# A fused attention, expert layer and convolution layer on one core: the first v split on GpSimd, DMA issues in another order, idle products in the routing, and a first copy in halves

## The chip, the cores and the metric

The kernel runs on one core of one Trainium2 chip. The metric is the device time of one execution in microseconds (us), the median of several runs. Five instruction streams run beside each other: TensorE (PE; its weight loads are shown apart as PEld), VectorE (DVE), ScalarE (ACT), GpSimd (POOL) and SyncE (SP), which here only issues DMA transfers. An instruction starts when those ahead of it in its own stream have been issued and the semaphores that it waits for have come. ACT and POOL issue DMAs too, each on its own queue (ACTq, POOLq; SP's is SPq).

## The reference, cut to what matters

Three layers follow each other. The attention has 4 batches of 8 heads, 576 positions and 64 columns, with a decay bias:

```python
scores = scale * np.matmul(q, k.transpose(0, 1, 3, 2))
cum = np.cumsum(np.maximum(s, 0.0), axis=-1)
bias = -(cum[:, :, :, None] - cum[:, :, None, :])
scores = np.where(causal, -1000000000.0, scores + np.minimum(bias, 0.0))
attn = exp(scores - max(scores));  attn = attn / (sum(attn) + 1e-09)
x = attn @ v                                   # heads joined: 4 x 576 x 512
logits, gate = x @ w_gate, sigmoid(x @ w_local)
e = argmax(logits[b, s]) if s == 0 or gate[b, s] < 0.5 else prev_e
y[b, s] = softmax(logits[b, s])[e] * (relu(x[b, s] @ w1[e]) @ w2[e])   # 8 experts, 512 -> 1024 -> 512
h = relu(y @ w_in);  out = (h * sigmoid(conv3(h))) @ w_out             # conv along s, 3 taps
```

Everything is float32. The kernel holds most operands as two float16 parts, a high one and the remainder.

## The kernel before

The attention goes through 8 units of 4 heads (`u` 0 to 7; two units are one batch). For each unit k and q come in by SP (`load`, tiles `st`), are split in high and low parts (`split_hi` on ACT, `split_lo` on GpSimd or DVE, tile `h` or in place in `st`), are transposed by two DMAs of SP (`turn`, written `k<-h` or `k<-st` in the trace) and copied into the second operand tile by DVE (`copy`, L290). `extra` lays the decay rows into the operand tile by two DMAs (`k<-ex`). There are three such operand tiles, `K1[0]` to `K1[2]`, and `constants` fills their constant rows by three memsets; `K1[2]` (named `k_143` in the order) first serves unit 2.

A unit needs a first pass, **stage a** (`za`, L391, reduced by DVE at L394 and L423), which finds each row's maximum. `max_turn` turns the maxima on PE (`mt`, L460), `max_out` copies them on ACT (`mr`, L465) and `max_row` writes them by DMA into a row of the operand tiles: two DMAs `k<-mr` (L472) for the heads' full blocks, one `t<-mr` (L475) for the last 64 positions, the tail. All went by SP, except the tail row of unit 0, which ACT issued. Only behind these can `scores` (`z`, L494 and L522) be taken; then come exp on ACT, the low part `plo` on DVE (L550) and the products with v (`o`, L566). Stage a of unit u+1 runs in pieces among the scores of unit u.

v comes in once for a batch by `loadv`: for batch 0 the first half (heads of unit 0) by GpSimd's queue, the second half (unit 1) by SP, 8 DMAs `nv` and 4 `nvt`. `split_v` (L337 on) scales v and takes the two parts `vv` and `vvt`, and a float32 copy `v0` of one block. For unit 0 ACT made the high parts (L351), DVE the low ones (L355) and GpSimd `v0`; for the later units GpSimd makes all, seven operations.

The order is written out by hand: every task gets a time in steps in `PAR` (`start` for the opening; `at` for the splits, transposes and extra rows of a unit, counted back from the unit's first step), and tasks are emitted sorted by it. On each engine the order of emission is the order of execution. `busy` puts out products that nobody reads, two ahead of each of the first eight scores.

Behind the attention `Routing.finish` picks an expert for each position: the last turned tile (`xT`, `xTt`), `logits` (L966, L971), the recurrence over positions (`nrp`, `rfp` on PE, a scan `er` on DVE, `ep` back on PE), ranks in each expert (`rk`), and index sums (`ix`, L1084) from which `rows` makes `idx`, the list of rows to gather. `warm` puts out products between (L1094, `w1` = 6 and `w2` = 8 of them). The expert layer works in blocks of 128 rows: `gather` (GpSimd, indirect, tile `xg`), `turn` (8 transposing products `xp` at L1258, one ACT copy `xt` at L1259), `mm1` (`hp`, L1228), `mm2`. ACT and DVE meanwhile split the experts' weights (tile `r`, L1159 and L1170). The last layer, `moe2`, follows.

Of the kernel before, what the change touches and what calls it, by code (L numbers as in the profile page):

```python
# [21 lines left out]
NB = 27  # L22
# [19 lines left out]
def bc(ap, shape):  # L42
    return ap.to_broadcast(shape)


class Keep:
# [7 lines left out]
 'u2': {'at': (-22.5, -21.5, -19, -18.9, -18), 'cp': (-14, -13), 'lv': -11, 'sv': -2, 'pa': -12, 'pn': 7, 'mx': -6},  # L54
 'u3': {'load': -35, 'loadq': 0, 'at': (-33, -30, -28, -27, -26.9), 'cp': (-22, -21), 'sv': -1, 'pa': -20, 'pn': 14, 'mx': -6},
# [52 lines left out]
           'ctq': 3.3,  # L108
           'c2': 3.5,
           'pt': 4.8,  # L110
           'mtt': 5.8,
           'sv0': 5.85,
           'mot': 5.9,
           'mrt': 5.95,
           'z': 6.0,
           'lv1': 7.5},
 'r': {'cut': 12, 'w1': 6, 'w2': 8, 'w3': 6},
# [7 lines left out]
def attention(tc, ctx, q, k, v, s, xd, rt, hook):  # L125
# [212 lines left out]
    def split_v(u):  # L338
        b, o = u // 2, u % 2 * NH
        a, t = U[b, "v"][:, o:o + NH], U[b, "vt"][:, o // 2:o // 2 + 2]  # L340
        w = U[u, "vv"] = vp.tile([128, NH, 4, 2, 65], F16, name="vv")
        wt = U[u, "vvt"] = vp.tile([128, NH // 2, 2, 65], F16, name="vvt")
        v0 = U[u, "v0"] = vp.tile([128, NH, 65], F32, name="v0")
        for x in (w, wt):
            i = (slice(None),) * (len(x.shape) - 2)
            G.memset(x[i + (0, slice(64, 65))], 1.0)
            G.memset(x[i + (1, slice(64, 65))], 0.0)
        G.memset(v0[:, :, 64:65], 1.0)
        for x, dh, dl in ((a, w[:, :, :, 0, 0:64], w[:, :, :, 1, 0:64]), (t, wt[:, :, 0, 0:64], wt[:, :, 1, 0:64])):
            if u == 0 or not PAR["h"]["vg"]:  # L350
                A.activation(dh, x, AF.Copy, scale=VS)  # L351
            else:
                G.tensor_scalar(dh, x, VS, 0.0, op0=ALU.mult, op1=ALU.add)
            if u == 0:
                V.scalar_tensor_tensor(dl, in0=x, scalar=VS, in1=dh, op0=ALU.mult, op1=ALU.subtract)  # L355
            else:
                G.tensor_scalar(x, x, VS, 0.0, op0=ALU.mult, op1=ALU.add)
                G.tensor_tensor(dl, x, dh, op=ALU.subtract)
        G.tensor_scalar(v0[:, :, 0:64], a[:, :, 0], VS if u == 0 else 1.0, 0.0, op0=ALU.mult, op1=ALU.add)
# [15 lines left out]
    def busy(z, n):  # L375
        for _ in range(n):
            PE.matmul(z.rearrange("p (x c) -> p x c", c=128), lhsT=id16, rhs=bc(id16[:, None], [128, 4, 128]), start=True, stop=True, skip_group_check=True)
# [89 lines left out]
    def max_row(u, hs=slice(0, 4), tails=True):  # L467
        n, Q = 0, nc.sync if u or hs else nc.scalar
# [15 lines left out]
    def scores(x):  # L484
# [4 lines left out]
        if 1 <= steps.index(x) <= 8:  # L489
            busy(z, 2)  # L490
# [194 lines left out]
    def second_a(r):  # L685
# [4 lines left out]
        lv0=lambda: loadv(0, 0, G), c2=lambda: (constants(G, K1[2]), tctx.close()),  # L690
# [101 lines left out]
class Routing:  # L792
# [210 lines left out]
    def finish(self, ctx, busy, between, behind):  # L1003
# [9 lines left out]
        z = T("z", [128, 512], pool=ps)  # L1013
        self.logits(NU - 1, z)
        self.collect(NU - 1)
        nrp, rfp = T("nrp", [128, 1024], pool=ps), T("rfp", [128, 1024], pool=ps)
# [4 lines left out]

        nrs, er = T("nrs", [128, S]), T("er", [128, S], F16)
# [22 lines left out]
        rk = T("rk", [128, 2, 8, 20], pool=ps)  # L1045
        PE.matmul(rk[:, 1], lhsT=self.ones, rhs=of, start=True, stop=True, skip_group_check=True)
        PE.matmul(rk[:, 0], lhsT=self.later, rhs=of, start=False, stop=True, skip_group_check=True)
        V.tensor_tensor(ex, ex, o, op=ALU.mult)
# [31 lines left out]
        ix, ixs = T("ix", [128, 5, NB], pool=ps), T("ixs", [128, 2, NB])  # L1080
# [153 lines left out]
def moe(tc, xd, yd, m, w_in, w_out, keep, splits, room, weights, xgp, xtp, unit):  # L1234
# [3 lines left out]
    with ExitStack() as ctx:  # L1238
# [14 lines left out]
        def turn(b):  # L1253
# [5 lines left out]
            A.activation(t, z, AF.Copy)  # L1259
# [409 lines left out]
```

## Time and profile before

| | |
|---|---|
| median of 3 runs | 684.68 us (684.28 to 685.42) |
| the profiled execution | 686.55 us, its span 684.3 us |
| PE busy | 623.9 us, 91% of the span |
| DVE busy | 451.0 us, 66% |
| ACT busy | 393.2 us, 57% |
| POOL busy | 255.4 us, 37% |
| attention, to the last turned tile | about 0 to 225 us |
| routing, to the first expert product | about 225 to 248 us |
| expert layer | about 248 to 508 us |
| last layer | about 508 to 684 us |

The span runs from the first to the last instruction on the core; 2.25 us of the profiled time lie around it. A busy share is an average over stages with different limits. In rows of the timeline "[2.98 <-DMA t<-mr]" says that the engine stood idle for 2.98 us ahead of this instruction, and what ended the wait. PEclk is TensorE's granted clock as a share of full speed; it has two levels, 1.2 GHz (0.50) and 2.4 GHz (1.00), so a mean between them is a stretch with both.

### The profile page before, as it was taken

To read this page: it belongs to the slowest core of one execution; us is meant where nothing else is said; L and a number is where in the kernel's file an instruction comes from. 1 tells how busy PE (TensorE), PEld (TensorE's weight loads), DVE (VectorE), ACT (ScalarE), POOL (GpSimd) and SP (SyncE) were. 2 spreads that over 40 slices of the span, in tenths; PEclk is the share of its full clock that TensorE was granted. 3 is DMA by queue.
4 is the path that set the end of the run, shared out by engine and by line. 5 is a ranking of instruction groups with operands and counts; after the bars stand their busy time and mean duration, and the time that the engine had idled before them with its cause. 6 is when DMAs were issued, how large, how long until landed. Compare 5 with 4: busy or idle time off the path is not lost. (4 is left out here: it accounts for less than half of the span.)

```text
span 684.3 us, 15451 instructions
## 1 busy us (share of the span) xinstructions
PE 623.9 (91%) x5177; PEld 390.1 (57%) x5177; DVE 451.0 (66%) x861; ACT 393.2 (57%) x661; POOL 255.4 (37%) x369
## 2 busy tenths in 40 slices
PE   6758899899999389899999989999899999999997
PEld 3437688778888244344444434444477766565443
DVE  7788888898765798475858486753059993645000
ACT  5656588687797837465637363632069975554111
POOL 8988966572350089612543434333000000000000
PEclk9989999999999689999999999999999999999999
DMA  7877866956655258999999999962471300000111
GB/s 173 169 163 132 151 141 129 156 101 137 219 146 214 60 185 234 249 364 235 263 353 192 335 175 238 202 152 67 104 128 29 71 16 32 16 31 32 47 61 48
DMA packets 168921, 101.80 MB, mean 149 GB/s; under 512 B 119808, under 2 KB 147112, under 8 KB 168828
## 3 DMA queue, kind: packets, MB, share of 16 engines
q1 hardware_dynamic: 164712, 88.65, 54.8%
q0 software_dynamic: 4112, 12.00, 5.8%
q8 instruction: 47, 0.77, 0.5%
q14 instruction: 46, 0.38, 0.2%
q10 hardware_dynamic: 4, 0.00, 0.0%
HBM read 62.18 MB, written 15.31 MB: 113 GB/s over the span
## 5 line engine op out<-in xcount | busy, mean ns | idle before, releaser
L1228 PE MATMUL hp<-r,xt 128*128 x504 | 113.9, 383 | 9.9 <-ACT xt L1259 8.1
L1228 PE MATMUL yp<-r,ht 128*128 x504 | 112.2, 379 | 1.6 <-PEq L1342 1.6
L1503 PE MATMUL o<-wo,g 128*128 128x512 f16 x432 | 94.5, 379 | 0.0
L1228 PEld LDWEIGHTS <-xt 128*128 128x128 f16 x504 | 49.6, 99 | 70.6 <-ACT xt L1259 11.3
L1455 PEld LDWEIGHTS <-wi 128*128 128x128 f16 x768 | 75.1, 98 | 21.9 <-issue 1.7
L1228 PEld LDWEIGHTS <-ht 128*128 128x128 f16 x504 | 48.6, 98 | 57.3 <-issue 2.6
L1170 DVE SCALAR_TENSOR_TENSOR r<-st,r 128x512 f32 (+3 forms) x80 | 71.0, 949 | 9.6 <-ACT r L1159 8.3
L1455 PE MATMUL hp<-yt,wi 128*128 128x288 f16 x576 | 71.9, 286 | 0.0
L1291 POOL DMA_INDIRECT yd<-ys,idx x21 | 21.9, 1044 | 132.0 <-DVEq L1212 77.1
L1159 ACT ACTIVATE r<-st 128x512 f32 (+3 forms) x84 | 57.4, 761 | 23.8 <-SPq L1221 16.0
L1503 PEld LDWEIGHTS <-g 128*128 128x128 f16 x432 | 42.3, 98 | 49.5
L538 ACT ACTIVATE phi<-z,lnes 128x512 f16<-128x512 f32 (+1 forms) x80 | 50.7, 634 | 34.1 <-PE z L497 33.7
L394 DVE TENSOR_REDUCE mx<-za 128x1 f32<-128x384 f32 (+4 forms) x93 | 54.5, 601 | 15.2 <-PE za L391 14.6
L550 DVE TENSOR_TENSOR plo<-z,phi 128x512 f16<-128x512 f32 (+1 forms) x80 | 48.1, 602 | 9.6 <-ACT z L539 8.1
L494 PE MATMUL z<-k 128*128 128x128 f16 (+2 forms) x320 | 48.6, 275 | 5.7 <-DVE plo L550 2.5
L539 ACT ACTIVATE z<-z,lnes 128x512 f32<-128x512 f32 (+1 forms) x80 | 48.7, 608 | 0.0
L1472 DVE SCALAR_TENSOR_TENSOR c<-hb,cw,c 128x576 f32<-128x576 f32 x32 | 26.1, 816 | 33.2 <-ACT c L1466 33.2
L1506 ACT ACTIVATE s<-o 128x512 f32<-128x512 f32 x18 | 10.7, 596 | 61.4 <-PE o L1503 61.4
L566 PE MATMUL o<-v,p 128*128 128x65 f32 x256 | 44.0, 283 | 0.0
L1289 ACT ACTIVATE ys<-yp,pp 128x512 f16<-128x512 f32 x21 | 14.4, 684 | 49.3 <-PE yp L1228 29.9
L1306 DVE TENSOR_SCALAR f<-s 128x256 int32<-128x256 int32 x32 | 11.6, 361 | 45.0 <-POOL wo L1315 16.1
L566 PE MATMUL o<-vv,phi 128*128 128x65 f16 (+1 forms) x512 | 41.1, 200 | 0.0
(299 smaller groups left out, 1236.5 us busy)
## 6 DMA issues: line engine op xcount, KB each, us to landing
st<-in_moe_w_dram SPq DMA_DIRECT2D x8, 2048.0 KB
st<-in_moe_w_dram SPq DMA_DIRECT2D x24, 512.0 KB
out_dram<-s SPq DMA_DIRECT2D x18, 256.0 KB
st<-in_k_dram SPq DMA_DIRECT2D x16, 256.0 KB
st<-in_q_dram SPq DMA_DIRECT2D x16, 256.0 KB
xd<-xh SPq DMA_DIRECT2D x16, 256.0 KB
k<-in_moe_w_dram SPq DMA_DIRECT2D x8, 512.0 KB
s<-in_moe_w_in_dram SPq DMA_DIRECT2D x16, 256.0 KB
```

The costliest lines, as they stand in the source:

```text
L394: return lambda: V.tensor_reduce(out, z.rearrange("p (e c) -> p e c", e=m), axis=AX.X, op=ALU.max)
L494: PE.matmul(out, lhsT=ks[i], rhs=qs[i], start=first and not i, stop=False, skip_group_check=True)
L538: A.activation(hi[:, 0:n], z[:, 0:n], AF.Exp, bias=lnes, scale=1.0 / SC)
L539: A.activation(p[:, 0:n], z[:, 0:n], AF.Exp, bias=lnes, scale=1.0 / SC)
L550: (V if md == "a" else G).tensor_tensor(lo[:, 0:n], p[:, 0:n], hi[:, 0:n], op=ALU.subtract)
L566: PE.matmul(out, lhsT=w, rhs=x, start=first, stop=last, skip_group_check=True)
L1159: i = self.nc.scalar.activation(hi, src, AF.Copy, scale=self.scale[w])
L1170: i = nc.vector.scalar_tensor_tensor(lo, in0=src, scalar=sc, in1=hi, op0=ALU.mult, op1=ALU.subtract)
L1228: i = self.nc.tensor.matmul(out, lhsT=lhsT, rhs=self.rings[w][:, c, k, bass.ds(s, 1), f], **kw)
L1455: PE.matmul(st[x][:, n, 0:HN], lhsT=wi[:, c, k, m], rhs=t[:, n, a + k], start=k + a + c == 0, stop=k == 3 and a == 4)
L1472: V.scalar_tensor_tensor(c, in0=h[:, 1:S + 1], scalar=cw[:, m, 1:2], in1=c, op0=ALU.mult, op1=ALU.add)
L1503: PE.matmul(o, lhsT=g[:, a, k, 128 * i:128 * i + 128], rhs=wo[:, c, k], start=j == 0, stop=j == 23)
```

## The change

Four things change.

- **The first v.** `split_v` puts all seven operations on GpSimd for unit 0 too; its task moves from 5.85 to 3.4. The memsets of `K1[2]` move behind the splits of unit 2 (`c3` at 6.6).
- **Issues in another order.** The tail row of unit 0 goes by SP. The second half of v is loaded at 5.98 instead of 7.5, the dump of zeros into `xd` at 8.0 instead of 6.0. Unit 2's extra rows go behind unit 1's maximum rows, unit 3's split of k behind the second v split.
- **Idle products.** `finish` puts out 3, 4, 5, 2 and 12 products into a tile `W` of its own, a whole PSUM bank that later holds `ix`; `w2` falls from 8 to 2. The eighth begin step has 5 `busy` products instead of 2.
- **The first copy.** `xt` of block 0 is copied in two halves.

```diff
- 'u2': {'at': (-22.5, -21.5, -19, -18.9, -18), 'cp': (-14, -13), ...
- 'u3': {'load': -35, 'loadq': 0, 'at': (-33, -30, -28, -27, -26.9), ...
+ 'u2': {'at': (-22.5, -21.5, -19, -18.9, -15.8), 'cp': (-14, -13), ...
+ 'u3': {'load': -35, 'loadq': 0, 'at': (-30.9, -30, -28, -27, -26.9), ...
...
+           'sv0': 3.4,
            'c2': 3.5,
+           'c3': 6.6,
...
-           'sv0': 5.85,
...
-           'z': 6.0,
-           'lv1': 7.5},
- 'r': {'cut': 12, 'w1': 6, 'w2': 8, 'w3': 6},
+           'lv1': 5.98,
+           'z': 8.0},
+ 'r': {'cut': 12, 'w1': 6, 'w2': 2, 'w3': 6},
...
-            if u == 0 or not PAR["h"]["vg"]:
-                A.activation(dh, x, AF.Copy, scale=VS)
-            else:
-                G.tensor_scalar(dh, x, VS, 0.0, op0=ALU.mult, op1=ALU.add)
-            if u == 0:
-                V.scalar_tensor_tensor(dl, in0=x, scalar=VS, in1=dh, op0=ALU.mult, op1=ALU.subtract)
-            else:
-                G.tensor_scalar(x, x, VS, 0.0, op0=ALU.mult, op1=ALU.add)
-                G.tensor_tensor(dl, x, dh, op=ALU.subtract)
+            G.tensor_scalar(dh, x, VS, 0.0, op0=ALU.mult, op1=ALU.add)
+            G.tensor_scalar(x, x, VS, 0.0, op0=ALU.mult, op1=ALU.add)
+            G.tensor_tensor(dl, x, dh, op=ALU.subtract)
...
-        n, Q = 0, nc.sync if u or hs else nc.scalar
+        n, Q = 0, nc.sync
...
-            busy(z, 2)
+            busy(z, 5 if steps.index(x) == 8 else 2)
...
+        W = T("ix", [128, 512], pool=ps)
+
+        def idle(n):
+            for _ in range(n):
+                PE.matmul(W.rearrange("p (x c) -> p x c", c=128), lhsT=self.id16, rhs=bc(self.id16[:, None], [128, 4, 128]), start=True, stop=True, skip_group_check=True)
+
+        idle(3)
         self.logits(NU - 1, z)
         self.collect(NU - 1)
+        idle(4)
...
+        idle(5)
...
+        idle(2)
         PE.matmul(rk[:, 1], lhsT=self.ones, rhs=of, start=True, stop=True, skip_group_check=True)
         PE.matmul(rk[:, 0], lhsT=self.later, rhs=of, start=False, stop=True, skip_group_check=True)
+        idle(12)
...
-        ix, ixs = T("ix", [128, 5, NB], pool=ps), T("ixs", [128, 2, NB])
+        ix, ixs = W[:, 0:5 * NB].rearrange("p (i n) -> p i n", n=NB), T("ixs", [128, 2, NB])
...
-            A.activation(t, z, AF.Copy)
+            for r in (slice(0, 4), slice(4, 8)) if b == 0 else (slice(0, 8),):
+                A.activation(t[:, r], z[:, r], AF.Copy)
```

On **SP**, between the transposes of unit 1 and those of unit 2 (tile `h` to `k`), the issues stood like this before. `k_142` is unit 1's operand tile, `k_143` unit 2's, `t_144` the tail's; `st` are the loads of k, q and k of units 2 and 3.

```order
L286 DMA k_142<-ex 3x2x1024 x2
L702 DMA xd<-zero 512x1x256
L170 DMA st_112<-in_k_dram 128x4x128 x2
L170 DMA st_112<-in_q_dram 128x4x128 x2
L170 DMA st_111<-in_k_dram 128x4x128 x2
L180 DMA nv<-in_v_dram 64x4x64 x8
L184 DMA nvt<-in_v_dram 32x2x64 x4
L282 DMA_TRANSPOSE k_717<-h 128x32x64 x2
L286 DMA k_143<-ex 3x2x1024 x2
L472 DMA k_142<-mr 1x8x128 x2
L475 DMA t_144<-mr 1x2x128
```

After, they stand like this.

```order
L287 DMA k_142<-ex 3x2x1024 x2
L470 DMA t_144<-mr 1x2x128
L181 DMA nv<-in_v_dram 64x4x64 x8
L185 DMA nvt<-in_v_dram 32x2x64 x4
L171 DMA st_112<-in_k_dram 128x4x128 x2
L171 DMA st_112<-in_q_dram 128x4x128 x2
L171 DMA st_111<-in_k_dram 128x4x128 x2
L697 DMA xd<-zero 512x1x256
L283 DMA_TRANSPOSE k_722<-h 128x32x64 x2
L467 DMA k_142<-mr 1x8x128 x2
L470 DMA t_144<-mr 1x2x128
L287 DMA k_143<-ex 3x2x1024 x2
```

The tail row of unit 0 is new here, v stands ahead of the loads and the zeros behind them, and the two extra rows went from between the transposes and unit 1's maximum rows to behind those.

On **POOL**, from the low part of unit 1's q on, before (`k_143` are the memsets of `K1[2]`, the pairs of `st` the low parts of unit 2's k and q and unit 3's k):

```order
L273 TENSOR_TENSOR st_111<-st_112,st_111 128x16x64
L210 MEMSET k_143 128x2x512
...
L272 TENSOR_SCALAR st_111<-st_111 128x1024
L273 TENSOR_TENSOR h<-st_111,h 128x16x64
...
L359 TENSOR_SCALAR v_588<-nv 128x4x64
L272 TENSOR_SCALAR st_112<-st_112 128x1024
L273 TENSOR_TENSOR h<-st_112,h 128x16x64
L272 TENSOR_SCALAR st_112<-st_112 128x1024
L273 TENSOR_TENSOR st_111<-st_112,st_111 128x16x64
...
L353 TENSOR_SCALAR vv<-nv 128x16x64
```

And after:

```order
L274 TENSOR_TENSOR st_111<-st_112,st_111 128x16x64
...
L351 TENSOR_SCALAR vv<-nv 128x16x64
L352 TENSOR_SCALAR nv<-nv 128x1024
L353 TENSOR_TENSOR vv<-nv,vv 128x16x64
L351 TENSOR_SCALAR vvt<-nvt 128x2x64
...
L354 TENSOR_SCALAR v_525<-nv 128x4x64
L273 TENSOR_SCALAR st_111<-st_111 128x1024
L274 TENSOR_TENSOR h<-st_111,h 128x16x64
L273 TENSOR_SCALAR st_112<-st_112 128x1024
L274 TENSOR_TENSOR h<-st_112,h 128x16x64
L211 MEMSET k_143 128x2x512
...
L351 TENSOR_SCALAR vv<-nv 128x16x64
```

The first v split takes the place of the memsets, which stand behind unit 2's q now; the low part of unit 3's k follows the second v split.

On **PE**, in the routing from the last of `ep` to the first index sum, before:

```order
L1038 MATMUL ep<-sel,er 32x32
L1046 LDWEIGHTS ones
L1046 MATMUL rk<-oh,ones 128x160
L1047 LDWEIGHTS later
L1047 MATMUL rk<-oh,later 128x160
L1084 LDWEIGHTS one
L1084 MATMUL ix<-bq,one 128x54
```

And after, where the pair in front stands twice and the pair behind `rk` twelve times:

```order
L1042 MATMUL ep<-sel,er 32x32
L1013 LDWEIGHTS unit
L1013 MATMUL ix<-unit 128x512
...
L1051 MATMUL rk<-oh,ones 128x160
L1052 LDWEIGHTS later
L1052 MATMUL rk<-oh,later 128x160
L1013 LDWEIGHTS unit
L1013 MATMUL ix<-unit 128x512
...
L1090 LDWEIGHTS one
L1090 MATMUL ix<-bq,one 128x54
```

The products go into the bank of `ix` and are what PE does while DVE makes `one`.

## Rows read from the trace of the kernel before

**Rows 1.** Three stretches: each engine's busy time, then PEclk, DMA share, GB/s.

```profile
42.75:49.35 6.60, 4.93 (x30) 3.58 (x31) 5.55 (x9) 1.78 (x4) 4.77 (x9) 0.50 0.69 140
...
83.70:226.50 142.80, 133.55 (x2093) 116.15 (x2091) 114.93 (x302) 114.16 (x217) 66.80 (x97) 1.00 0.65 157
226.50:243.50 17.00, 7.89 (x76) 4.37 (x73) 13.60 (x55) 11.92 (x18) 1.73 (x2) 0.51 0.06 12
```

**Rows 2.** Timeline of PE, opening: start, duration, instruction, idle before and its releaser.

```profile
40.20 0.63 PE L522 MATMUL z<-t,k 128*128 128x64 f16 x16 [2.98 <-DMA t<-mr]
44.13 0.61 PE L391 MATMUL za<-k 127*128 127x128 f16 x4 [3.31 <-DVE k L290]
...
61.37 0.59 PE L494 MATMUL z<-k 128*128 128x512 f16 x2 [1.35 <-DMA k<-mr]
```

**Rows 3.** Timeline of DVE, opening.

```profile
36.77 2.93 DVE L355 SCALAR_TENSOR_TENSOR vv<-nv,vv 128x1024 f16<-128x1024 f32 x1 [1.19 <-ACT vv L351]
...
40.14 3.94 DVE L290 COPY k<-k 64x2048 f16<-64x2048 f16 x2
...
61.70 1.25 DVE L290 COPY k<-k 64x2048 f16<-64x2048 f16 x1
```

**Rows 4.** Timeline of ACT, the issue of the tail row.

```profile
37.16 1.20 ACTq L475 DMA_DIRECT2D t<-mr  x1
```

**Rows 5.** Timeline of POOL, opening.

```profile
30.70 2.95 POOL L210 MEMSET k<- 128x1024 f32 x3
...
41.09 2.44 POOL L273 TENSOR_TENSOR h<-st,h 128x1024 f16<-128x1024 f32 x1
...
48.73 1.04 POOL L353 TENSOR_SCALAR vv<-nv 128x1024 f16<-128x1024 f32 x1 [1.26 <-DMA nvt<-in_v_dram]
```

**Rows 6.** Timeline of SP's issues, opening.

```profile
34.20 1.67 SPq L286 DMA_DIRECT2D k<-ex  x2
...
40.21 6.76 SPq L180 DMA_DIRECT2D nv<-in_v_dram  x8
...
49.63 6.94 SPq L282 DMA_TRANSPOSE k<-h  x2
...
58.78 1.38 SPq L472 DMA_DIRECT2D k<-mr  x2
...
62.00 7.10 SPq L282 DMA_TRANSPOSE k<-st  x2
...
71.36 5.44 SPq L180 DMA_DIRECT2D nv<-in_v_dram  x8
```

**Rows 7.** Timeline of PE, routing and first expert products.

```profile
225.87 0.75 PE L966 MATMUL z<-w,xT 128*128 128x9 f16 x24 [0.69 <-ACT xTt L949]
...
238.42 1.37 PE L1084 MATMUL ix<-bq,one 128*128 128x54 f16 x20 [5.32 <-DVE one L1071]
...
244.64 1.90 PE L1094 MATMUL z<-r,unit 128*128 128x512 f16 x8
246.38 0.61 PE L1258 MATMUL xp<-unit,xg 128*128 128x128 f16 x8
248.24 2.10 PE L1228 MATMUL hp<-r,xt 128*128 x9 [1.25 <-ACT xt L1259]
```

**Rows 8.** Timeline of DVE, routing.

```profile
224.99 0.69 DVE L947 CAST xT<-z 128x512 f16<-128x512 f32 x1 [0.15 <-PE z L946]
...
229.95 1.35 DVE L1030 TENSOR_TENSOR_SCAN er<-nrs,rfp 128x576 f16<-128x576 f32 x1 [1.18 <-PE rfp L1020]
...
245.83 0.18 DVE L1113 TENSOR_TENSOR ixs<-ixs,ix 128x27 f32<-128x27 f32 x1
```

**Rows 9.** Timeline of ACT, the first copy of turned rows.

```profile
247.08 1.02 ACT L1259 ACTIVATE xt<-xp 128x1024 f16<-128x1024 f32 x1 [7.26 <-issue]
```

**Rows 10.** Timeline of POOL, the first gather, and the tile's view.

```profile
241.47 1.10 POOL L1251 DMA_INDIRECT xg<-xd,idx  x1 [29.61 <-DVE pc L1101]
...
DMA to landing us min/median/max: 3.5/6.1/7.6
```

More of the change, by code (lines that the diff above doesn't have):

```diff
@@ L53 @@
 PAR = {'u1': {'sv': -3, 'pa': -7, 'pn': 4, 'mx': -4},
- 'u2': {'at': (-22.5, -21.5, -19, -18.9, -18), 'cp': (-14, -13), 'lv': -11, 'sv': -2, 'pa': -12, 'pn': 7, 'mx': -6},
- 'u3': {'load': -35, 'loadq': 0, 'at': (-33, -30, -28, -27, -26.9), 'cp': (-22, -21), 'sv': -1, 'pa': -20, 'pn': 14, 'mx': -6},
+ 'u2': {'at': (-22.5, -21.5, -19, -18.9, -15.8), 'cp': (-14, -13), 'lv': -11, 'sv': -2, 'pa': -12, 'pn': 7, 'mx': -6},
+ 'u3': {'load': -35, 'loadq': 0, 'at': (-30.9, -30, -28, -27, -26.9), 'cp': (-22, -21), 'sv': -1, 'pa': -20, 'pn': 14, 'mx': -6},
  'u': {'load': -51,
@@ L349, in split_v @@
         for x, dh, dl in ((a, w[:, :, :, 0, 0:64], w[:, :, :, 1, 0:64]), (t, wt[:, :, 0, 0:64], wt[:, :, 1, 0:64])):
-            if u == 0 or not PAR["h"]["vg"]:
-                A.activation(dh, x, AF.Copy, scale=VS)
-            else:
-                G.tensor_scalar(dh, x, VS, 0.0, op0=ALU.mult, op1=ALU.add)
-            if u == 0:
-                V.scalar_tensor_tensor(dl, in0=x, scalar=VS, in1=dh, op0=ALU.mult, op1=ALU.subtract)
-            else:
-                G.tensor_scalar(x, x, VS, 0.0, op0=ALU.mult, op1=ALU.add)
-                G.tensor_tensor(dl, x, dh, op=ALU.subtract)
-        G.tensor_scalar(v0[:, :, 0:64], a[:, :, 0], VS if u == 0 else 1.0, 0.0, op0=ALU.mult, op1=ALU.add)
+            G.tensor_scalar(dh, x, VS, 0.0, op0=ALU.mult, op1=ALU.add)
+            G.tensor_scalar(x, x, VS, 0.0, op0=ALU.mult, op1=ALU.add)
+            G.tensor_tensor(dl, x, dh, op=ALU.subtract)
+        G.tensor_scalar(v0[:, :, 0:64], a[:, :, 0], 1.0, 0.0, op0=ALU.mult, op1=ALU.add)
     def block(t, n, h, i):
@@ L689, in attention @@
     begin_tasks = dict(
-        lv0=lambda: loadv(0, 0, G), c2=lambda: (constants(G, K1[2]), tctx.close()),
+        lv0=lambda: loadv(0, 0, G), c2=tctx.close, c3=lambda: constants(G, K1[2]),
         thk=lambda: tail_hi("k"), thq=lambda: tail_hi("q"), tlk=lambda: tail_lo("k"), tlq=lambda: tail_lo("q"),
```

## The prediction

> **What bounds the kernel now.** I read the stretches by engine first, then the timeline of PE in the two places that the change touches, and from each wait there the row of the engine that ended it.
>
> In the opening PE has three waits [rows 2]: 2.98 us for the tail row of unit 0 (ended at 40.20), 3.31 us for DVE's copy of unit 1's k (44.13), 1.35 us for unit 1's maximum rows (61.37). Behind the first two the granted clock is 0.50 for 6.6 us [rows 1]. From 83.70 to 226.50 PE is busy for 133.55 of 142.80 us, 94%, at full clock [rows 1]: that stretch is bound by PE, so what the opening wins ahead of it reaches the routing.
>
> The routing, 226.50 to 243.50, is a chain of small steps between DVE and PE: PE is busy for 7.89 of 17.00 us, at a clock of 0.51 [rows 1]. It ends with the first expert product at 248.24 [rows 7]. Ahead of that stand the transposing products `xp` at 246.38, behind eight warm products (244.64, 1.90 us) and behind DVE's last reading of a PSUM bank, at 245.83 for 0.18 us [rows 7, 8], though the gather, issued at 241.47 and 3.5 us on the way at the least [rows 10], had landed at about 244.97.
>
> **The first v.** DVE loses `vv` (2.93 us, 36.77) and the smaller `vvt`; its copies of k, at 40.14 for 3.94 us [rows 3], can start where DVE began to wait for ACT, 36.77 - 1.19 = 35.6, or when k has landed, which I put at 36. Their own price has two ends: 2 x 1.25 = 2.5 us as at 61.70, and 3.94 us as at 40.14 [rows 3]. So they end between 38.5 and 39.9 and stage a of unit 1 starts at 39 to 40 instead of 44.13, some 4 to 5 us earlier. ACT loses the high part, about the 1.19 us that DVE waited, so the tail maximum is ready at about 36.0 and SP, whose extra rows end at 34.20 + 1.67 = 35.9 [rows 6], issues the row there. On ACT's queue it took from 37.16 to 40.20, 3.04 us [rows 2, 4]; SP's maximum rows take from 59.47 (the second of the two at 58.78) to 61.37, 1.9 us [rows 2, 6]. The tail scores start at 37.9 to 39.0, about 2 us earlier.
>
> GpSimd pays: two passes at 1.04 and one at 2.06 to 2.44 for `vv` [rows 5] (the upper end is the subtraction at 41.09), 4.1 to 4.5 us, with the small tiles 5 to 6 us. In front the three memsets (2.95 us at 30.70) [rows 5] go away to a later place, so unit 2's q, which ended at 41.09 + 2.44 = 43.5, moves by -0.5 to +3 us. Its reader, SP's transposes, starts at 49.63 [rows 6]: 6 us of cover, so I cost it at nothing. Without that cover it would be those 3 us. Three more busy products at the eighth step cost 3 x 0.24 us on PE (1.90 / 8) [rows 7] in a stretch where PE waits for DVE's reductions: 0 to 0.7 us, taken at 0.
>
> What is late next is SP. Its sum from 34.20 on: extra rows to 35.9, tail row (half of 1.38, 0.7) to 36.6, v 5.44 us (as at 71.36, no loads just ahead) to 6.76 us (as at 40.21), the zeros and loads that filled 35.9 to 40.21, 4.3 us, the small v loads with the gap behind them, 46.97 to 49.63, 2.7 us [rows 6]. That gives 49.0 to 50.3 for the transposes. I take 49.0, 0.6 earlier than before, since the loads that stood ahead of v now stand behind it. The transposes last 6.94 us, and the maximum rows now follow at once, at about 56.0 instead of 58.78, since unit 2's extra rows, which filled the 2.2 us between, went behind them. That is 2.8 us, or 1.5 if the transposes start at 50.3. Stage a starts 4 us earlier, so its maxima wait for SP and not SP for them.
>
> The rows show no transfer that is issued directly behind transposes, so whether it is held by their data isn't seen; the 2.2 us that lay between bound it from above and zero from below. The Trainium skill, DMA: Bandwidth & Descriptors, Queues, rings and completion order, says that each DMA engine starts the descriptors of one queue in order; by it the maximum rows lie behind the transposes' data, and the term would be 0.6 (2.8 - 2.2) instead of 2.8 us.
>
> Unit 3 takes some of it back: its transposes start at 62.00 [rows 6] behind a q split on GpSimd, which has up to 3 us more in front, so they hardly move, and the scores of units 1 and 2 run up to them. I take 2.0 us for the opening, bounds 0.6 and 2.8.
>
> One rule speaks against the move. First the rows: the copies of k took 1.97 us each beside a subtraction on GpSimd (41.09 to 43.53), and 1.25 at 61.70 [rows 3, 5]. The Trainium skill, SBUF — State Buffer, on the shared port pair, calls it an exclusive lock: a DVE operation of certain kinds and one of GpSimd don't share it, the second is blocked to the end of the first. The trace fits that in direction. By it each copy could wait for a whole subtraction, 2 x (1.25 + 2.44) = 7.4 us, and end at 43.4; stage a would come 0.7 us earlier, the maximum rows at 57 or so instead of 56.0, and the opening would be worth 1.0 instead of 2.0.
>
> **The routing.** A product of 512 columns is 0.24 us at full clock (1.90 / 8), twice that at half. The three idle ones start when DVE has emptied their bank, 224.99 + 0.69 = 225.68 [rows 8], so the logits go from 225.87 [rows 7] to 226.4: 0.5 later. If PE's clock then stays at full, the four (1.0 us), five (1.2), two (0.5) and twelve (2.9 us of a wait of 5.32) [rows 7] end inside waits that were there, and the small products between them run at twice the speed: the scan waited 1.18 us for PE [rows 8], of which I expect 0.5 back, the ranks 0.4, the index sums (1.37 us) [rows 7] 0.2 to 0.6. The gather's list comes 0 to 1.0 us earlier, taken 0.5.
>
> Then the bank is no longer shared, and the warm products are two instead of eight. `xp` waits for the gather alone, 244.97 - 0.5 = 244.5 instead of 246.38: 1.9 earlier (1.4 where the chain gains nothing). The first half of the copy releases PE up to 0.5 us sooner (half of 1.02) [rows 9]; from `xp` to the first expert product 1.86 us pass [rows 7], of which the copy is the end, so I take 0.1 of it. The first expert product comes at about 246.3. Its weights' low parts are DVE's work, which moves only by those 0.5 us, and PE runs up to DVE, ACT and the gathers later in the layer; I let 0.4 be lost there: 1.6 us, bounds 1.0 and 2.2.
>
> **Sum.** 2.0 + 1.6 = 3.6 us. The profiled execution, 686.55 us, lies 1.87 above the median; the terms are differences, so it would go to 683.0 and the median from 684.68 to 681.1. I say 681.2.
>
> **Rivals.** First, the opening is not worth anything: SP's issues come at the late end, or the maximum rows are held behind the transposes' data. For it speaks that one queue carries both, against it that 2.2 us of extra rows no longer stand between. Then only the routing counts: 683.0.
>
> Second, the idle products don't hold the clock. Before, it falls at about 226.5, behind the waits around the turn of the last tile, which the change leaves as they are; only three products and the logits lie between. If it falls all the same, four products take 1.9 us where 1.0 were covered, five 2.4 against 1.4, two 1.0 against 0.5, twelve 5.8 against 5.3: with the 0.5 of the logits about 2.9 us later on the chain, less 2.2 since `xp` no longer waits behind bank and warm products. The routing is 0.7 us slower, the sum -1.3: 683.4. This is the case in which the change doesn't do what it says. The Trainium skill, TensorE: Matmul & The Clock Gate, Part 1, says that activity releases the throttle, which speaks for the forecast; how much is enough here no row shows.
>
> Third, slower: PE reaches unit 1's scores early and then stands still for some 3 us ahead of the maximum rows, a wait longer than the 1.35 us of before. After 2.98 and 3.31 us of waiting the clock was at half for 6.6 us [rows 1, 2]. That decides if PE is what the chain waits for behind 58.5: half of 6.6, up to 3.3 us, lost, -2.0 + 3.3 = +1.3, and with the routing at +0.7 the time is 686.7.
>
> Fourth, more: unit 3 is not in the way, the chain in the routing is 1.0 us shorter and the expert layer keeps all: 2.8 + 2.2 = 5.0, 679.7.
>
> **How the numbers follow.** The forecast has 0.55, with its own range 680.2 to 682.6; the first rival 0.17, the second 0.13, the third 0.08, the fourth 0.07. The range, 679.3 to 684.2, leaves out the third and the tails. By 0.2% (1.4 us, about what a measurement of this kernel can tell from no change) the bound of faster is 683.3: forecast and fourth rival, 0.62, and half of the first two, 0.15, give 0.77; the other half 0.15, with a part of the third 0.16; slower 0.07.
>
> **What would show it.** In the timeline of PE the tail scores at about 38, stage a of unit 1 at 39 to 40, the first full scores of unit 1 behind the maximum rows at about 58.7; granted clock 1.00 instead of 0.50 in 42.75 to 49.35; SP's transposes at 49.0. In the routing a clock near 1.00 from 226.5 on, `xp` at about 242.5 and the first expert product at 244.3 on the new trace, where the opening's 2.0 us are already off. Wrong would be a new wait of PE ahead of 58.5 with a half clock behind it, an `xp` that waits for another thing than the gather, or an expert layer that gives back more than 0.4 us.

## The result and the profile after

The changed kernel is slower: 689.25 us median (684.65 to 694.71, 20 runs) against 684.89 (20 runs of before beside it), a ratio of 1.0057 with a 95% interval of 1.0036 to 1.0077. The forecast was 681.2 with a range of 679.3 to 684.2. The profiled execution took 688.71 us, its span is 687.0. Medians here and below are of all executions; the ratios are taken over the executions, so they differ a little from the quotients of the medians (e4's most), and leave out four that were disturbed as a whole (two of e11, its profiled one among them, one of e7, one of the kernel before). Each kernel has one profiled execution, so a number from a trace tells where that execution spent its time.

The windows of the changed kernel, columns as in [rows 1], answer to those there; the first line is the kernel before in a window that is not shown there:

```profile
49.35:80.40 31.05, 25.73 (x341) 20.69 (x340) 27.02 (x63) 18.59 (x33) 27.69 (x58) 0.99 0.72 128
...
42.75:49.35 6.60, 5.63 (x60) 3.87 (x59) 5.93 (x14) 0.80 (x2) 6.24 (x11) 1.00 0.57 154
49.35:80.40 31.05, 20.95 (x265) 17.83 (x264) 17.88 (x37) 17.56 (x31) 27.53 (x49) 0.84 0.86 156
...
226.50:243.50 17.00, 13.99 (x96) 6.96 (x96) 10.18 (x38) 12.33 (x20) 0.00 (x0) 0.70 0.22 57
```

The clock is whole in 42.75 to 49.35, as forecast, and falls later: 0.84 in the stretch behind, which was at 0.99 before. In the routing it is 0.70 (0.51 before). The timeline of PE in the opening, for [rows 2]:

```profile
37.75 0.63 PE L517 MATMUL z<-t,k 128*128 128x64 f16 x16 [0.38 <-DMA t<-mr]
38.21 0.39 PE L386 MATMUL za<-k 127*128 127x128 f16 x4
...
49.23 0.40 PE L455 MATMUL mt<-ident,mx 128*18 128x128 f32 x2
...
62.16 1.04 PE L489 MATMUL z<-k 128*128 128x512 f16 x2 [8.86 <-DMA k<-mr]
...
68.05 0.41 PE L386 MATMUL za<-k 127*128 127x128 f16 x4
```

Two waits of 2.98 and 3.31 us became 0.38 and nothing, stage a starts 5.9 us earlier and its maxima are turned at 49.23. Then PE stands idle for 8.86 us, for unit 1's maximum rows, and goes on 0.8 us later than before. What follows runs at half clock: two products of 512 columns take 1.04 instead of 0.59 us. SP's issues, for [rows 6]:

```profile
36.77 6.17 SPq L181 DMA_DIRECT2D nv<-in_v_dram  x8
42.99 2.01 SPq L185 DMA_DIRECT2D nvt<-in_v_dram  x4
45.04 0.98 SPq L171 DMA_DIRECT2D st<-in_k_dram  x2
...
48.67 1.11 SPq L697 DMA_DIRECT2D xd<-zero  x1
49.97 8.51 SPq L283 DMA_TRANSPOSE k<-h  x2
58.58 1.77 SPq L467 DMA_DIRECT2D k<-mr  x2
...
63.74 7.22 SPq L283 DMA_TRANSPOSE k<-st  x2
```

SP issues with hardly a gap from 34 to 71 us, in this kernel as in the one before. The transposes begin 0.3 us later than before and take 8.51 instead of 6.94 us; the maximum rows go out at 58.58 (58.78 before), and unit 3's transposes 1.7 us later than before. In the routing, for [rows 7] and [rows 8], PE and DVE's scan:

```profile
229.90 1.44 PE L1013 MATMUL ix<-unit 128*128 128x512 f16 x3 [0.35 <-DVE xT L942]
...
232.63 1.89 PE L1013 MATMUL ix<-unit 128*128 128x512 f16 x4
234.31 0.86 PE L1023 MATMUL nrp<-unit,znr 128*128 128x128 f16 x5
...
252.55 0.61 PE L1264 MATMUL xp<-unit,xg 128*128 128x128 f16 x8
253.98 2.75 PE L1234 MATMUL hp<-r,xt 128*128 x12 [0.82 <-ACT xt L1266]
```
```profile
236.05 1.35 DVE L1034 TENSOR_TENSOR_SCAN er<-nrs,rfp 128x576 f16<-128x576 f32 x1 [1.69 <-PE rfp L1023]
```

The first idle products run at 0.48 us each, half clock, and the scan waits 1.69 us for PE where it waited 1.18. The first expert product comes 5.7 us later than before: 4.2 of that lies ahead of the last cast of the turned tile (229.16 against 224.99), 1.6 behind. The last layer begins 2.7 us later (519.20 against 516.52) and takes 167.8 us in both.

Two of these numbers are within what single executions differ by. The expert layer, from its first product to the last layer, took 265.2 us here and 268.3 before; in the runs below without e14 and e15 it takes from 262.4 (e6) to 268.7 us (e10), though its products behind the first block are the same, and e2, which starts it 4.4 us late, takes 268.2. So it is not shown that it took 3 us back. From the last cast to the first expert product the routing of before took 23.25 us in its own profile, but up to 24.74 in others that have it (e2); the changed kernel's 24.82 is hardly beyond that.

### The profile page after: what moved, and what is told of

The parts are those of the page before. It is cut to its first block, busy times and chain, and to the rows that moved or that the text cites. A ratio compares the mean times of both kernels' runs of the same rounds, so it can differ in the third digit from the quotient of the medians.

```text
span 687.0 us, 15502 instructions
## 1 busy us (share of the span) xinstructions
PE 633.1 (92%) x5200; PEld 395.2 (58%) x5200; DVE 445.2 (65%) x859; ACT 391.9 (57%) x660; POOL 259.0 (38%) x375
## 5 line engine op out<-in xcount | busy, mean ns | idle before, releaser
L561 PEld LDWEIGHTS <-phi 128*128 128x128 f16 x544 | 40.9, 108 | 0.0
```

The source lines that it names most:

```text
L561: PE.matmul(out, lhsT=w, rhs=x, start=first, stop=last, skip_group_check=True)
```

## Experiments on the two halves of the change

Every ratio is against the kernel before on the same chip. The first pair takes the parts one by one.

**e1, the routing's part alone**: the kernel before with `W`, the five `idle` calls, `'w2': 2` and the halves.

> The kernel before with the routing's part of the change alone (idle products, the bank of their own, two warm products for eight, the copy in halves); the opening is untouched. In the changed kernel the scan `inc` came 6.8 us later than before, while the attention ended 3.9 us later, so 2.8 us were lost between. Theory A, the idle products overrun because the clock falls all the same: granted clock about 0.6 to 0.75 in the stretch behind the last turned tile, the scan `inc` 2 to 3 us later against the last turned tile than before, the first expert product about 0.5 to 1.8 us later, the whole within 0 to 2 us of the kernel before. Rival B, the half clock there came only with the late opening: the idle products keep the clock near 1.0, the first expert product comes 1.5 to 2 us earlier, the whole is 1 to 2 us faster.

Measured: 687.16 us against 686.23, ratio 1.0003 (0.9970 to 1.0036). From the last cast (225.86) the scan `inc` is reached after 10.53 us, before after 8.15; the first expert product after 24.20 (before 23.25). Clock 0.70. Theory A holds in the trace: the products overrun at half clock, and the scan comes 2.4 us later, where the other executions with the routing of before lie between 8.15 and 8.63. The 24.20 us lie within their 23.25 to 24.74, and no cost shows at the end.

**e2, the opening's part alone**: the changed kernel with the routing and the copy put back.

> The kernel before with the opening's part of the change alone (v split on GpSimd, issues in the other order, three more busy products); the routing is untouched. Theory A, the opening lost what the attention lost, 3.9 us, and the expert layer takes back a part of it: a wait of PE of 8 to 9 us for unit 1's maximum rows, clock at half behind it, the attention 3 to 4.5 us later, the whole 2 to 4.5 us slower. Rival B, the expert layer swallows it, since its own chain of loads sets its end: the same wait, but the whole within 1 us of the kernel before.

Measured: 689.32 against 686.23, ratio 1.0045 (1.0023 to 1.0067); the wait is 9.11 us. Theory A holds: the loss is the opening's, and the expert layer gave none of it back (268.2 us).

**The opening's runs** in one table: start of unit 1's first full scores; time from there to stage a of unit 2; from there to the turn of its maxima; the turn of unit 7's maxima, the last; ratio. The opening of before is also in e1, e4 and e8, and gives a measure of how far single executions differ: unit 1's scores at 60.87 to 61.53, the last maxima at 190.70 to 192.56.

| | unit 1 scores | to stage a | to its maxima | last maxima | ratio |
|---|---|---|---|---|---|
| before | 61.37 | 3.09 | 15.70 | 191.91 | |
| changed | 62.16 | 5.89 | 16.12 | 195.86 | 1.0057 |
| e2 | 62.61 | 5.88 | 16.37 | 194.85 | 1.0045 |
| e3 | 60.18 | 4.29 | 17.65 | 194.13 | 1.0035 |
| e5 | 62.99 | 3.09 | 16.36 | 193.91 | 1.0061 |
| e6 | 58.26 | 5.86 | 16.65 | 192.40 | 1.0008 |
| e7 | 60.93 | 5.86 | 17.36 | 195.61 | 1.0010 |
| e9 | 61.25 | 5.88 | 17.52 | 195.74 | 1.0023 |
| e10 | 59.97 | 3.24 | 18.45 | 194.82 | 1.0012 |
| e12 | 61.67 | 3.09 | 17.50 | 193.84 | 1.0037 |
| e13 | 62.69 | 5.85 | 16.16 | 196.44 | 1.0022 |
| e14 | 58.24 | 4.80 | 22.45 | 198.19 | 1.0139 |
| e15 | 58.48 | 4.60 | 23.57 | 198.43 | 1.0150 |

The last two columns do not rank the runs alike: e7 has its last maxima at 195.61 and a ratio of 1.0010, e12 has 193.84 and 1.0037.

**e3, transposes first**: e2 with the loads of unit 3 ahead, unit 4's k and the zeros behind unit 1's maximum rows.

```diff
-                plan(max(t0 + c["load"], 7), lambda u=u: load(u, "k"))
+                plan(5.9 if u == 3 else max(t0 + c["load"], 12.15), lambda u=u: load(u, "k"))
...
-           'z': 8.0},
+           'z': 12.3},
```

> The opening alone as in the run before it, but the loads of unit 3's k and q go ahead of the second half of v, and the load of unit 4's k and the zeros behind unit 1's maximum rows: nothing large stands directly ahead of unit 2's transposes. Theory A, the maximum rows were late because unit 2's transposes queue behind loads and zeros on the one queue: the transposes start at 46 to 48 and take about 7 us instead of 8.5, the maximum rows let PE go on at 56 to 58 instead of 62.2, the wait is 3 to 5 us instead of 8.9, and the whole is 2 to 5 us faster than the opening alone. Rival B, the rows wait for the transposes' own data wherever these stand and unit 3 is the next late thing: the wait shrinks, the whole does not move by more than 1 us.

Measured: 688.33 against 686.23, ratio 1.0035 (1.0011 to 1.0060). The transposes start at 47.25 and take 7.37, but the two loads now stood ahead of the tail row too:

```profile
42.98 1.01 PE L517 MATMUL z<-t,k 128*128 128x64 f16 x16 [5.53 <-DMA t<-mr]
```

Issued from 38.35 to 38.97 behind 1 MB of loads, its 0.5 KB took 4.0 us more to arrive. Stage a came late by that. Neither theory is decided by it.

**e6, the tail row first**: e3 with 5.96 for 5.9, which puts the tail row ahead of the loads.

> The opening alone with SP's issues in this order: extra rows, tail row of unit 0, loads of unit 3's k and q, second half of v, unit 2's transposes, unit 1's maximum rows, then unit 4's k and the zeros. Against the run e3 only the tail row goes ahead of the two loads (there it landed 4 us after its issue, at 42.98, behind 1 MB of loads). Theory A, what lies on the one queue ahead of a small transfer sets when it lands: the tail scores at 38 instead of 43, unit 1's maxima ready by 52, the maximum rows issued at 53 to 55, unit 1's first scores at 55.5 to 57.5 (62.6 in the opening alone, 61.4 before), the whole 2 to 5 us faster than the opening alone. Rival B, unit 3's transposes, which cannot move, take it all back: unit 1's scores as in A, unit 2's maxima at 80 or later, the whole within 1 us of the kernel before.

Measured: 685.20 against 684.98, ratio 1.0008 (0.9983 to 1.0034). SP and PE:

```profile
47.69 7.82 SPq L283 DMA_TRANSPOSE k<-h  x2
...
55.62 1.45 SPq L467 DMA_DIRECT2D k<-mr  x2
...
62.47 7.26 SPq L283 DMA_TRANSPOSE k<-st  x2
```
```profile
58.26 1.01 PE L489 MATMUL z<-k 128*128 128x512 f16 x2 [4.70 <-DMA k<-mr]
```

The order of SP's issues is what the opening lost by: with it mended the loss against before is within the interval, here and in e7 and e10 below (1.0010 and 1.0012), which have the same order. But nothing is won: unit 1 starts 3.1 us earlier, 2.8 go in the half clock behind the 4.7 us wait and 0.95 in unit 2's stretch. Both theories have a part: A in the opening, B in the whole.

**e12, two numbers alone**: the kernel before with `lv1` 5.98 and `z` 8.0.

> The kernel before with one edit: the second half of v loaded at 5.98 and the zeros at 8.0, so that SP issues v ahead of the loads of units 3 and 4 and of the zeros. The split of v stays on ACT and DVE. Theory A, the loads directly ahead of the transposes cost by themselves: the transposes take 8 us or more instead of 6.94, the maximum rows are issued at 60 or later (58.78 before, with unit 2's extra rows still between), unit 1's scores come at 62.5 to 64, the whole 1 to 3 us slower. Rival B, the order alone does no harm and only the split of v with it does: transposes and scores within 0.6 us of before, the whole within 1 us.

Measured: 687.95 against 684.95, ratio 1.0037 (1.0016 to 1.0059). So the order costs by itself. But not as theory A has it: the transposes take 7.25 us with the same loads and zeros just ahead as in the changed kernel, and the scores come at 61.67, 0.3 later.

```profile
46.76 2.32 SPq L702 DMA_DIRECT2D xd<-zero  x1
49.69 7.25 SPq L282 DMA_TRANSPOSE k<-h  x2
```

In this trace the loss is further on. Unit 3's k, loaded behind v, makes ACT wait 4.11 us and GpSimd 4.94 us; GpSimd's row is then 2 us later, and its subtraction for unit 4 (71.94 before) falls on DVE's copy of unit 3, two engines in turn:

```profile
73.98 2.13 POOL L273 TENSOR_TENSOR h<-st,h 128x1024 f16<-128x1024 f32 x1
```
```profile
74.28 2.38 DVE L290 COPY k<-k 64x2048 f16<-64x2048 f16 x1 [0.22 <-DMA k<-st]
...
78.78 0.66 DVE L290 COPY k<-k 64x2048 f16<-64x2048 f16 x1
```

The copy takes 2.38 us where the next takes 0.66, and unit 2's reductions behind it are late by 2.0 us, the last maxima by 1.9. That this is what the 1.0037 consists of is not shown: the profiled execution took 682.89 us, 5.1 less than the median of e12, and made the loss up in the expert layer (263.1 us).

**e9, v and zeros at their old places**: e2 with `lv1` 7.5 and `z` 6.0.

> The opening alone, but with the second half of v and the zeros at their old places: SP issues extra rows, tail row of unit 0, zeros, the loads of units 3 and 4, then v, then unit 2's transposes, then unit 1's maximum rows. All else of the opening's part stays (v split on GpSimd, tail row by SP, extra rows of unit 2 behind the maximum rows). Theory A, the loads and zeros directly ahead of the transposes are what made these slow (8.2 to 8.5 us instead of 6.9): here they take 6.9 to 7.2 us from about 50, the maximum rows are issued at 57 to 57.6, unit 1's first scores come at 59.5 to 60.5 (62.6 in the opening alone), and the whole is 1 to 3 us faster than the opening alone, 0 to 2 us slower than the kernel before. Rival B, the loss is in another part (GpSimd's longer row, the extra rows behind): transposes short, but unit 2's row maxima at 83 or later and the whole as slow as the opening alone.

Measured: 688.38 against 685.55, ratio 1.0023 (0.9996 to 1.0050). The transposes take 7.08, as theory A says, and the rows let PE go on at the time of before (theory A had 59.5 to 60.5), yet 4.5 us are lost by the turn of unit 2's maxima, which is rival B's sign:

```profile
61.25 1.04 PE L489 MATMUL z<-k 128*128 128x512 f16 x2 [7.77 <-DMA k<-mr]
```

2.8 of them are the half clock (5.88 against 3.09 in the table), 1.8 are in unit 2's stretch: in this trace the earlier stage a by itself only bought a longer wait. The interval of the time holds no change.

**e5 and e11, products in the wait**: e2 and e9 with `busy(z, 36)` and `busy(z, 32)` ahead of unit 1's first scores.

> The opening alone with 36 products of 512 columns put out ahead of unit 1's first scores, so that TensorE works through the 9.1 us wait for the maximum rows instead of standing idle; nothing else differs from the opening alone (688.7 us span). Theory A, the half clock behind the wait costs about 2 of the 3 to 4 us lost: granted clock about 1.0 from 50 to 70 instead of 0.78 in 49.35 to 80.40, unit 1's first scores at 62.2 to 62.8 as before, unit 2's row maxima turned at about 82.5 instead of 84.9, the attention 1.5 to 2.5 us earlier than in the opening alone. Rival B, the loss sits in SP's later issues for unit 3: the clock is whole, but unit 2's maxima stay at 84 to 85 and the time stays within 1 us of the opening alone.

> The run e9 (opening alone, v and zeros at their old places) with 32 products of 512 columns in TensorE's wait for unit 1's maximum rows. In e9 unit 1's scores came at 61.25, as in the kernel before (61.37), yet unit 2's row maxima were turned at 84.65 instead of 80.16. Theory A, that loss is the half clock behind the wait: clock near 1.0 from 49 to 80 instead of 0.78, unit 1's scores at 61 to 62, unit 2's maxima at 80.5 to 82, the attention's end 2 to 4 us earlier than in e9 and the whole 1 to 3 us faster than e9. Rival B, unit 3's transposes, 1.9 us later there than before, and GpSimd's longer row hold the pace: clock whole, unit 2's maxima still at 83.5 or later, the whole within 1 us of e9.

Measured: e5 688.83 against 684.98, ratio 1.0061 (1.0040 to 1.0081); e11 690.13 against 684.95, ratio 1.0058 (1.0034 to 1.0081). In e5 the clock is whole and the stretch behind the scores is that of before; the 36 products leave no gap ahead of the scores, so they may outlast the wait a little:

```profile
49.35:80.40 31.05, 26.59 (x309) 19.75 (x307) 19.56 (x44) 18.91 (x33) 28.87 (x59) 1.00 0.86 151
```

Unit 2's maxima come 2.4 us earlier than in e2, the last maxima 0.9, the whole not at all. In the time rival B holds, in e11 too: with the wait filled neither is faster than its partner (1.0045 and 1.0023). In e5's profile 2.0 us are lost at the last maxima and 3.2 at the first expert product (251.44), which lies within the interval of its ratio (2.7 to 5.5 us).

**e13, a longer row on SP**: the kernel before with the zeros in four DMAs instead of one, the same bytes.

> The kernel before with the zeros for the spare rows issued as four DMAs of a quarter each instead of one; the bytes are the same. SP's row grows by three issues of some 0.64 us, 1.9 us, ahead of unit 2's transposes. Theory A, SP's row sets the pace of the opening: unit 2's transposes start at 51 to 51.7, unit 3's at 63.4 to 64, unit 2's row maxima are turned 1.5 to 3 us later than 80.16, and the whole is 1.5 to 3 us slower. Rival B, SP has slack and the loss of the change lies in GpSimd's, DVE's or TensorE's part: unit 3's transposes later, but unit 2's maxima within 0.7 us and the whole within 1 us of the kernel before.

Measured: 687.46 against 685.59, ratio 1.0022 (0.9992 to 1.0051). In its profile unit 2's transposes begin at 50.70 and unit 3's at 63.31, a little ahead of theory A's bounds, and the opening of the kernel before, with its old v split, loses as the changed one does: a 4.00 us wait for the maximum rows, half clock, 4.5 us at the last maxima.

```profile
62.69 1.01 PE L494 MATMUL z<-k 128*128 128x512 f16 x2 [4.00 <-DMA k<-mr]
```

The trace speaks for theory A; the time points its way by 1.9 us, but its interval holds no change, so it isn't proven.

**e14, e15, a shorter row on SP**: e6 with unit 3's transposes planned earlier, unit 4's q and the zeros behind them, and the memsets of `K1[2]` on DVE; e15 with e8's routing on top.

> The opening as in e6, with SP's row up to unit 3's transposes made shorter: unit 4's q and the zeros are issued behind them, and the memsets of the third operand tile go from GpSimd (2.96 us) to DVE, which idles there, so that unit 3's q is split earlier. Theory A, unit 3's transposes set the pace: they start at 59.5 to 60.8 (62.0 before, 62.5 in e6), unit 2's row maxima are turned at 77 to 79.5 (80.2 and 80.8), the attention ends 1 to 2.5 us earlier than before and the whole is 0.5 to 2.5 us faster. Rival B, the next unit's k and q come too late instead: unit 3's transposes early, but ACT waits for unit 4's loads and the whole is within 1 us of the kernel before or slower.

> The opening of e14 with the routing of e8 (idle products, and nine more ahead of the last turn). Theory A, what the opening gains arrives: attention as in e14, the first expert product 1.2 us earlier against the last turned tile than in the kernel before, the whole 1 to 3.5 us faster than the kernel before. Rival B, the expert layer's loads give it back: within 1 us of the kernel before.

Measured: e14 695.15 against 685.59, ratio 1.0139 (1.0114 to 1.0165); e15 694.74, ratio 1.0150 (1.0115 to 1.0184). Unit 3's transposes start at 61.78, only 0.2 us earlier than before, so theory A's premise was not met. Rival B's wait came: ACT's row is in order as well, and it stood for the load that I had pushed behind:

```profile
engine line waited for: us in total, times, longest us
...
ACT h L265 <- DMA st<-in_q_dram: 6.8, 1, 6.8
```

Unit 2's stretch grew to 22.45 us: the load of unit 4's q could not be put off.

## Experiments on the routing, and both parts mended

**e4, the bank and the halves without idle products**: `W` for `ix`, `'w2': 2`, the copy in halves.

> The kernel before with the bank of its own for the index sums, two warm products for eight and the copy in halves, and with no idle product. Theory A, the idle products alone cost and these three gain: the chain of the routing as before, the products that turn the first rows wait for the gather alone and come 1 to 1.5 us earlier, the first expert product 1.2 to 1.9 us earlier, the whole 0 to 1.5 us faster. Rival B, the expert layer's own chain gives it back: the first expert product earlier, the whole within 0.5 us.

Measured: 684.72 against 686.23, ratio 0.9999 (0.9968 to 1.0030). The first expert product comes 22.35 us behind the last cast, 0.9 earlier than before. What came last ahead of `xp`:

```profile
242.74 1.41 PE L1085 MATMUL ix<-bq,one 128*128 128x81 f16 x20
...
244.23 0.60 PE L1095 MATMUL z<-r,unit 128*128 128x512 f16 x2
244.67 0.61 PE L1259 MATMUL xp<-unit,xg 128*128 128x128 f16 x8
```
```profile
244.49 0.61 PEld L1259 LDWEIGHTS <-xg 128*128 128x128 f16 x8 [0.15 <-DMA xg<-xd,idx]
```

PE works without a gap through the second index sums and two warm products, and the weight load for `xp` waits 0.15 us for the gather: sums and gather end together. The gain is there and small, below the forecast of theory A, and the whole does not show it.

**e8, the clock held**: e1 with nine products more in the 2.2 us ahead of the last turn.

```diff
+            for _ in range(hold):
+                nc.tensor.matmul(z, lhsT=self.id16, rhs=bc(self.id16[:, None], [128, 4, 128]), start=True, stop=True, skip_group_check=True)
             for i, b in enumerate(blocks):
```

> The routing alone as in e1, with nine products of 512 columns more in the 2.2 us in which TensorE waits for the last tile ahead of its turn. Theory A, the clock falls because of the waits around the last turn, and with these filled it stays: granted clock about 1.0 instead of 0.70 in the stretch behind, the three, four, five, two and twelve products end inside their waits, the scan of the ranks 2.5 to 3.5 us earlier against the last turned tile than in e1, the first expert product 3 us earlier than in e1. Rival B, the clock falls anyway, later: the chain is no more than 1 us shorter than in e1.

Measured: 684.17 against 684.98, ratio 0.9991 (0.9961 to 1.0021). Theory A's first half holds, the waits around the turn decide the clock; PE waited 0.26 us ahead of the last turn where it waited 2.21 before, and the idle products behind run at 0.26 us each:

```profile
226.17 0.81 PE L1020 MATMUL ix<-unit 128*128 128x512 f16 x3 [0.56 <-DVE xT L949]
...
227.97 1.04 PE L1020 MATMUL ix<-unit 128*128 128x512 f16 x4
229.16 0.82 PE L1030 MATMUL nrp<-unit,znr 128*128 128x128 f16 x5 [0.15 <-DVE znr L1000]
```
```profile
226.50:243.50 17.00, 12.99 (x116) 6.30 (x114) 12.89 (x54) 12.34 (x18) 1.10 (x1) 0.92 0.07 14
```

Its second half does not: `inc` comes 8.56 us behind the cast, 2.0 earlier than in e1, but not earlier than the 8.15 of before at half clock. The five `nrp` products take 0.82 us at full clock (1.00 from 226 to 234) and 0.86 in the changed kernel at half. The first expert product comes after 22.00 us, 1.25 earlier than before.

**e7 and e10, both parts**: e6 with e4's routing; e6 with 20 products in the wait and e8's routing.

> The opening of e6 with the bank of its own, two warm products and the copy in halves of e4, without idle products. Theory A, the two parts add: the first expert product against the last turned tile 1.4 us earlier than before, the attention's end as in e6; the whole 0 to 1.5 us faster than e6 and, if e6 gains 3 us against the kernel before, 3 to 4 us faster than it. Rival B, the expert layer's chain of loads sets its end: the first expert product earlier, but the whole within 0.7 us of e6.

> The changed kernel with three things mended: SP's order as in e6, 20 products in TensorE's wait for unit 1's maximum rows, nine in the wait ahead of the last turn as in e8. Theory A, with the queue in order and the clock held both parts of the change bring something: clock near 1.0 from 49 to 80 and from 226 on, the attention ends 0 to 2 us earlier than in the kernel before and the first expert product another 1 us earlier, the whole 1 to 3 us faster than the kernel before (4 to 7 us faster than the changed kernel). Rival B, unit 3's transposes and the expert layer's loads set the pace: the whole within 1 us of the kernel before.

Measured: e7 686.06 against 684.98, ratio 1.0010 (0.9988 to 1.0032); e10 686.89 against 685.55, ratio 1.0012 (0.9987 to 1.0036). In neither case theory A: neither beats the kernel before. In e7's profile the same order of issues let PE go on at 60.93 where e6 had 58.26: SP's row is 2 us longer from one execution to the next. In e10 unit 2 starts early and at full clock, and its stretch takes 18.45 us instead of 15.70.

## Why the prediction was wrong

- **The first v, tail row and stage a: right.** Tail scores at 37.75 (forecast 37.9 to 39.0), stage a at 38.21 (39 to 40), clock 1.00 in 42.75 to 49.35. The copies cost 0.80 and 0.94 us, below the lower bound of 1.25 and with no wait for whole subtractions. GpSimd's longer row did no harm to unit 2, as said.
- **SP's sum, the failing step of the opening.** I put the transposes at 49.0 with 6.94 us and the rows at 56.0; they came at 49.97, still within the bounds of 49.0 to 50.3, with 8.51 us and the rows at 58.58. The price of the transposes is the term that failed: 6.8 to 7.0 us in the five profiles with the old order (before, e1, e4, e8, e13), 7.1 to 8.5 in every other order. Loads just ahead of them do not explain it alone, since e12, with them, took 7.25 (behind zeros that took 2.32 instead of 0.64) and e6, e7 and e10, without them, 7.8 to 8.1; what makes the pair slow stays open. The rows then needed 2.5 us behind the last issue (59.66 to 62.16), not 1.9. A term of -2.8 measured +0.8. A small row can be late behind what was issued ahead of it: e3's tail row came 4.0 us after its issue behind 1 MB of loads, the changed kernel's 1.0 us after it with no loads ahead; that it is the one queue, and not the traffic of all, no run separates. The rule quoted from the Trainium skill (DMA: Bandwidth & Descriptors, Queues, rings and completion order) spoke against the forecast. This trace goes its way by the 0.6 us, not by the 2.2 that the prediction took from it.
- **The wait itself.** I took the time won by PE for the opening's gain, and left the clock to the third rival with 0.08. Its price was right (up to 3.3): 2.8 us, the same in six profiles, 5.85 to 5.89 us against 3.09. It should have been in the sum, since even the forecast had PE wait for about 3 us. The changed kernel's +4.0 us at unit 2's maxima is 0.8 for the late rows, 2.8 for the clock and 0.4 in the stretch behind. That the clock's part reaches the end is not shown: e5, which holds the clock, and e11, which fills the same wait, are no faster.
- **Unit 3.** "Hardly move" was wrong: 1.7 us later, and e12's trace shows how loads behind v reach DVE's copies by way of ACT and GpSimd. The order of two entries alone costs 1.0037 of the 1.0045 of the opening; e9, the opening without them, 1.0023, whose interval holds no change. The two add to 1.0060, within e2's interval.
- **The routing: the second rival happened.** The clock fell behind the last turn; the chain to `inc` took 2.6 us more than before, where the rival had 2.9, and the first expert product was 1.6 us later (0.7). The rival's sum was off: its five terms give 3.4 with the logits (2.9 without the twelve behind `inc`), and the credit of 2.2 is 1.5 by its own rows (1.4 for `xp`, 0.1 for the copy), so 1.9 and not 0.7. The step of the forecast that failed even with the clock held is that small products run at twice the speed: 0.82 against 0.86 us. And `xp` does not wait for the gather alone: in the changed kernel the second index sums and warm products at half clock come last and nothing waits for the gather, in e4 both end within 0.15 us. At the end no worth of the routing's part shows either way (1.0003, 0.9970 to 1.0036).
- **The expert layer.** The 0.4 us that I let it give back can be neither confirmed nor refused: it differs by 6 us from one profiled execution to the next. e4 and e8 came 0.9 and 1.25 us ahead at the first expert product, and the intervals of their times, some 2 us to either side, are too wide to show that.

What the runs leave open: why the transposes take longer in the new orders, why e5 and e11 with the wait filled are no faster at the end, and whether SP's row alone (e13) costs as much as its profile says.

## What to carry to other kernels

Before crediting an earlier start, follow it to the next queue that is full. Here SP issued with hardly a gap before and after, so time that PE won only lengthened its wait, and behind the waits of 4.0 to 9.1 us in six profiles the next stretch ran at half clock and took 2.8 us longer. A price of an issue holds for the order in which it was read: the same two transposes took 6.8 to 7.0 us in the old order and up to 8.5 in others. In a hand-written order a load that goes later delays every engine whose row is in order behind it. One profiled execution shows where its own time went; before a difference between two is read as an effect, see how far executions of one and the same part differ. Putting idle products in waits pays only if the work behind them is bound by the clock: small products were not.

## What was not expected of the hardware

A copy on DVE and a subtraction on GpSimd hardly overlap. The copy of unit 3 ends 0.55 to 0.57 us behind the end of a subtraction on GpSimd in four kernels, whenever it starts: before, 74.61 against 74.06; e6, 75.22 against 74.65; e12, 76.66 against 76.11; changed, 78.62 against 78.07. So it measured 0.81, 1.51, 2.38 and 1.21 us, where 0.65 stand without. In the opening of the changed kernel it went the other way round, GpSimd paid:

```profile
36.12 0.74 POOL L353 TENSOR_TENSOR vvt<-nvt,vvt 128x128 f16<-128x128 f32 x1
...
37.19 1.47 POOL L273 TENSOR_SCALAR st<-st 128x1024 f32<-128x1024 f32 x1
...
40.84 1.04 POOL L273 TENSOR_SCALAR st<-st 128x1024 f32<-128x1024 f32 x1
```

The first two run beside DVE's copies at 35.77 and 36.83 and take 0.74 and 1.47 us where 0.42 (the second v split) and 1.04 stand without. The Trainium skill (SBUF — State Buffer, on the shared port pair) calls the pair an exclusive lock that the first of the two keeps to the end of its instruction; these rows agree to some 0.1 us.
